# Attention and a gated feed-forward layer on one core: downward products three units behind instead of two, and the 64-key tile multiplied on 128 rows

## The chip, the cores and the metric

The kernel runs on one core of one Trainium2 chip. The metric is the device time of one execution in microseconds (us). The core has a matrix engine (PE, whose weight loads the profile lists apart as PEld), a vector engine (DVE), a scalar engine (ACT), a third elementwise engine (POOL) and a queue for transfers (SP). Each engine works through its own list of instructions in order; semaphores make one engine wait for another.

## What is computed

```python
# q, k, v: (8 batches, 8 heads, 576 positions, 64)
scores = q @ k.T / 8
mask = block_i >= block_j            # blocks of 64 positions, causal by block
attn = softmax(where(mask, scores, -1e9))
out = attn @ v                        # -> x: 4608 tokens x 512
h = x @ w_in                          # 512 -> 2048
g = h * erf(softplus(h))
result = g @ w_out                    # 2048 -> 512, float32
```

## The kernel before

**Attention** runs head by head (64 heads). For each head the scores are formed twice: once with queries on the rows, to find each row's maximum (`maxes`, L391 and L394), and once with keys on the rows (`probs`, L437 and L438), whose exponentials (L442) are the probabilities. The 576 keys make five tiles: four of 128 keys and one (`j` = 4) of 64. For two heads together `pv` multiplies the probabilities with the values (L486, output columns 64) and with a block of ones (L509, output columns 32), which gives the sums of the rows. The operand `V` holds one float32 array for the first three batches (`len(vv) == 1`), and from batch 3 on a high and a low float16 half (`len(vv) == 2`). There the lower 64 rows of the key tile of 64 are zero in the value array (padded on the host) and in the staged probabilities (a fill with zeros at L293). `min(P, S - j * P)` is the number of rows of the tile that the products of `pv` use: 128, and 64 for `j` = 4.

**The feed-forward layer** works on 18 tiles `t` of 256 tokens. The hidden 2048 are 16 slices of 128, two of which make a unit `u`; slices 0 to 7 are group 0 (units 0 to 3) and 8 to 15 group 1 (units 4 to 7). There are 144 units; `m16_4` in a name is tile 16, unit 4. A unit has three stages:

- up (L182): 24 products of 256 columns into one PSUM bank `h`;
- the gate (`gate`, L151 to L159): on ACT a tanh (L151) and two squares (L152, L153), on DVE four steps (L154 to L157, the last of which is the last reader of `h`), on ACT the rounding to float16 `gh` (L158), on POOL the rest `gl` (L159);
- down (L191): 12 products of 512 columns with `gh` and `gl` as the stationary operand, into the two output banks `o` of the tile.

`moe1` hands out these steps a few at a time between the steps of attention. It puts the up products of a unit together with the downward products of a unit that is `LAG` units older, in one merged list:

```python
downs.append(d)
lists.append((up, 0, 1))
if len(downs) > LAG or not jobs and downs:
    lists.append((downs.pop(0), 0, 1))
todo.extend(merged(*lists))
```

A scheduler then sets the order of each engine's list when the program is built, from the order of writing, priorities and times of its own; at run time each engine keeps to its list. While attention lasts, `h` has two banks (`ps_h`); once it is done, four (`ps_h2` is added), and only units of the feed-forward layer are left. Weights arrive as float64 and are converted in the first 20 heads or so (`to_f32`, `split_w`); the scale of each weight group comes from a small product `wt` (L125), which waits for a sum over all converted slices of the group (`wrs`, L123).

The lines on buffers: `mpool` has three buffers for each tag, so `gh`, `gl`, `r0` and `r1` have three each. `r0` and `r1` are the two float32 intermediates of the gate.

Of the kernel before, what the change touches and what calls it, by code (L numbers as in the profile page):

```python
# [8 lines left out]
F16 = mybir.dt.float16  # L9
F32 = mybir.dt.float32  # L10
# [22 lines left out]
def tile_attention_moe(ctx: ExitStack, tc: tile.TileContext, qk, v, w, maskrows, sels, out):  # L33
    nc = tc.nc
    B, H, D4, S = qk.shape
# [3 lines left out]
    P = 128  # L39
# [15 lines left out]
    cpool = ctx.enter_context(tc.tile_pool(name="cpool", bufs=1))  # L55
    wpool = ctx.enter_context(tc.tile_pool(name="wpool", bufs=1))
    xpool = ctx.enter_context(tc.tile_pool(name="xpool", bufs=2))
    mpool = ctx.enter_context(tc.tile_pool(name="mpool", bufs=3))
# [4 lines left out]
    make_identity(nc, ident)  # L63
    ones32 = cpool.tile([P, 32], F16, name="ones32")
    nc.gpsimd.memset(ones32, 1.0)
    ones = cpool.tile([P, P], F32, name="ones")
    nc.gpsimd.memset(ones, 1.0)
    bias = {}

    def const(val):  # L70
        if val not in bias:
            t = cpool.tile([P, 1], F32, name=f"c{len(bias)}")
            nc.gpsimd.memset(t, val)
            bias[val] = t
        return bias[val]
# [66 lines left out]
    def gate(h, name, t, g):  # L142

        nu = h.shape[1]
        n = nu * T
        flat = h.rearrange("p a b -> p (a b)")
        gh, gl = (mpool.tile([P, n], F16, tag=t_, name=f"{name}_{t_}") for t_ in ("gh", "gl"))
        r0, r1 = (mpool.tile([P, n], F32, tag=t_, name=f"{name}_{t_}") for t_ in ("r0", "r1"))
        r0s = r0.rearrange("p (a b) -> p a b", b=T)
        for b, lo, hi in spans(t * T, T):  # L150
            nc.scalar.activation(r0s[:, :, lo:hi], h[:, :, lo:hi], AF.Tanh, bias=const(p1), scale=bss[b][g][:, 0:1])  # L151
        nc.scalar.activation(r1, r0, AF.Square, bias=const(b1), scale=a1)  # L152
        nc.scalar.activation(r0, r1, AF.Square, bias=const(b2), scale=a2)  # L153
        nc.vector.scalar_tensor_tensor(out=r0, in0=r0, scalar=c3, in1=r0, op0=ALU.add, op1=ALU.mult)  # L154
        nc.vector.scalar_tensor_tensor(out=r0, in0=r1, scalar=c4, in1=r0, op0=ALU.add, op1=ALU.mult)  # L155
        nc.vector.scalar_tensor_tensor(out=r0, in0=r0, scalar=c5, in1=r0, op0=ALU.add, op1=ALU.mult)  # L156
        nc.vector.scalar_tensor_tensor(out=r0, in0=r0, scalar=fin, in1=flat, op0=ALU.add, op1=ALU.mult)  # L157
        nc.scalar.copy(gh, r0)  # L158
        nc.gpsimd.tensor_tensor(out=gl, in0=r0, in1=gh, op=ALU.subtract)  # L159
        return gh, gl  # L160

    def spans(t0, n):

        for b in range(t0 // S, (t0 + n - 1) // S + 1):
            yield b, max(0, b * S - t0), min(n, (b + 1) * S - t0)
# [49 lines left out]
            parts.append(x)  # L215
        return parts

    LAG = 2
    RATE = [12, 12, 28]
    done = []  # L220
    jobs = []
# [37 lines left out]
    def moe1(ready):  # L259
# [5 lines left out]
        if not todo:  # L265
            lists = []
            if jobs and len(done) >= 2 * jobs[0][2] + 2:
# [11 lines left out]
# [3 lines that stand above are left out]
# [4 lines left out]
    with tc.tile_pool(name="apool", bufs=2) as apool, tc.tile_pool(name="spool", bufs=1) as spool, \  # L286
# [14 lines left out]
        def bank(name):  # L301

            turn.append(0)
            k = len(turn) % 8 if not loaded else 0
            if k in (2, 5):
                return ps_h.tile([P, 512], F32, tag="h", name=name)
            if k in (3,):
                return ps_o.tile([P, 512], F32, tag="o", name=name)
            return ps_a.tile([P, 512], F32, tag="a", name=name)
# [151 lines left out]
        def pv(qd, pp, prs, V, usb, rs):  # L461

            vv = V[1:]
            terms = ((0, 0), (1, 0), (0, 1)) if len(vv) > 1 else ((0, 0),)
            one = ones32 if len(vv) > 1 else ones[:, :32]
            st = {}

            def ranges(q0, q1):

                for j in range(5):  # L470
                    if starts[j] < q1:
                        a = max(q0, starts[j])
                        pt, c = offs[j]
                        c += a - starts[j]
                        yield j, min(P, S - j * P), a - q0, pt, slice(c, c + q1 - a)

            def go(hf, j0, j1):
                q0, q1 = halves[hf]
                todo = list(ranges(q0, q1))
                if j0 == 0:  # L480
                    st[hf] = bank(f"u{qd}_{pp}_{hf}")
                u = st[hf]
                for j, kk, a, pt, cs in todo[j0:j1]:
                    for iv, ip in terms:
                        for hd in range(2):
                            nc.tensor.matmul(u[64 * hd : 64 * hd + 64, a : q1 - q0], lhsT=vv[iv][:kk, 2 * pp + hd, j, :], rhs=prs[hd][pt][ip][:kk, cs],  # L486
                                             start=j == 0 and (iv, ip) == terms[0], stop=j == todo[-1][0] and (iv, ip) == terms[-1])
                if j1 >= len(todo):
                    nc.scalar.copy(usb[:, q0:q1], u[:, : q1 - q0])


            order = []
            for hf, (q0, q1) in enumerate(((0, SH), (SH, S))):
                at, todo = 0, list(ranges(q0, q1))
                for n_, (j, kk, a, pt, cs) in enumerate(todo):
                    for k in range(len(vv)):
                        first, last = n_ == 0 and k == 0, n_ == len(todo) - 1 and k == len(vv) - 1
                        for hd in range(2):
                            order.append((at, hf, hd, k, kk, a, q1 - q0, pt, cs, first, last))
                        at += q1 - q0 - a  # L500
            order.sort(key=lambda o: o[0])

            def sums(n0, n1):
                if n0 == 0:
                    st["us"] = bank(f"us{qd}_{pp}")
                u = st["us"]
                for _, hf, hd, k, kk, a, w_, pt, cs, first, last in order[n0:n1]:
                    g = 2 * hf + hd
                    nc.tensor.matmul(u[32 * g : 32 * g + 32, a:w_], lhsT=one[:kk, :], rhs=prs[hd][pt][k][:kk, cs], start=first, stop=last)  # L509
                if n1 >= len(order):  # L510
                    nc.scalar.activation(rs[:, : S - SH], u[:, : S - SH], AF.Identity, bias=eps)
                    nc.scalar.activation(rs[:64, S - SH :], u[:64, S - SH : SH], AF.Identity, bias=eps[:64])

            return [lambda: go(0, 0, 2), lambda: sums(0, len(order)), lambda: go(1, 0, 5)]

        known = []
# [58 lines left out]
        vs, prs, usbs = {}, {}, {}  # L575
# [69 lines left out]
        for n in range(N + 3):  # L645
# [19 lines left out]
            if n % 2 == 0 and 2 <= n <= N:  # L665
                j = n // 2 - 1
                qd, pp = divmod(j, 2)
                usbs[j] = apool.tile([P, S], F32, tag="usb", name=f"usb{j}", bufs=2)
                steps = pv(qd, pp, [prs.pop(2 * j), prs.pop(2 * j + 1)], vs[qd], usbs[j], rss[j % 3])
                lists.append((late("pv", steps), 0, 1))  # L670
                if pp == 1:
                    normals[n + 1] = qd
# [60 lines left out]
```

## Time and profile before

| | |
|---|---|
| median of 3 runs | 1327.11 us (1323.97 to 1327.33) |
| profiled execution | 1333.15 us, of which the span of the core's instructions is 1331.3 us |
| mean granted PE clock | 0.973 of full speed |
| busy: PE, PEld, DVE, ACT, POOL | 1221.1, 804.8, 892.5, 784.6, 520.5 us |
| start of the first and last downward product | 164.6 and 1327.0 us |
| last product of attention (L566) | 1128.7 us |

The prediction quotes the rows themselves. In a row of a group, the columns are line, engine, operation, names and shapes, count, then busy time and mean duration of one in ns, then the engine's idle time just before such instructions and who ended it. In a row of waits they are who waited for whom, the time in total, the number of times and the longest. In a row of the timeline they are the start, the duration (over the whole of a merged run of instructions), engine, line, operation, count, and in brackets the idle time before it and who ended it. Ends of matrix products are modelled: a downward product shows some 0.38 us even where the next starts 0.22 us after it.

### The profile page before, as it was taken

What the parts mean: (1) busy time and instruction counts of PE and PEld (TensorE: products, weight loads), DVE (VectorE), ACT (ScalarE), POOL (GpSimd) and SP (SyncE); (2) the same over time, 40 slices, a digit from 0 to 9 for tenths busy, and PEclk for the clock granted to TensorE, in tenths of its full rate; (3) what the DMA queues carried; (4) which work ended last, traced back from release to release, by engine and by line L of the source; (5) the groups of instructions that cost most, each with busy time, mean ns of one, the idle gap of its engine ahead of it and who ended that gap; (6) DMA issues with size and microseconds to landing.
All of it is one profiled execution on the core that took longest, in us unless ns stands there. A gap on an engine that the chain in (4) does not pass through costs nothing. (4 is left out here: it accounts for less than half of the span.)

```text
span 1331.3 us, 23618 instructions
## 1 busy us (share of the span) xinstructions
PE 1221.1 (92%) x9108; PEld 804.8 (60%) x9108; DVE 892.5 (67%) x1583; ACT 784.6 (59%) x1555; POOL 520.5 (39%) x486
## 2 busy tenths in 40 slices
PE   1899898979999999999999999999999999999997
PEld 0455565556666676666666666667676666555553
DVE  4773887758567777686667766776778755554544
ACT  2453666557556676666666666666666675555553
POOL 4445445424434353534435343534343232222121
PEclk9899899779999999999999999999999999999999
DMA  9786568533444445454444544444434121211111
GB/s 264 190 215 149 128 180 198 146 94 91 119 114 108 121 121 123 112 114 110 101 129 104 123 113 108 117 125 107 120 97 111 55 66 37 86 56 48 64 48 48
DMA packets 95808, 151.74 MB, mean 114 GB/s; under 512 B 7804, under 2 KB 44988, under 8 KB 95696
## 3 DMA queue, kind: packets, MB, share of 16 engines
q1 hardware_dynamic: 69840, 93.34, 24.1%
q0 software_dynamic: 25216, 56.73, 20.0%
q8 instruction: 72, 1.18, 0.4%
q14 instruction: 40, 0.33, 0.1%
q10 hardware_dynamic: 640, 0.17, 0.1%
HBM read 121.73 MB, written 28.31 MB: 113 GB/s over the span
## 5 line engine op out<-in xcount | busy, mean ns | idle before, releaser
L182 PE MATMUL m_h<-xh,w 128*128 128x256 f16 x2304 | 474.2, 275 | 6.4 <-DVE m_r L157 5.2
L182 PEld LDWEIGHTS <-w 128*128 128x128 f16 x3456 | 326.7, 99 | 137.6 <-issue 17.6
L191 PE MATMUL o<-w,m_gh 128*128 128x512 f16 x1152 | 334.0, 387 | 27.4 <-ACT m_gh L158 25.2
L159 POOL TENSOR_TENSOR m_gl<-m_r,m_gh 128x512 f16<-128x512 f32 x144 | 174.7, 1213 | 424.1 <-ACT m_gh L158 382.5
L182 PE MATMUL m_h<-xl,w 128*128 128x256 f16 x1152 | 316.4, 275 | 0.9 <-DMA xl<-x_d 0.9
L394 DVE TENSOR_REDUCE mx<-s 64x1 f32<-64x288 f32 (+4 forms) x384 | 173.9, 470 | 122.6 <-PE s L391 121.6
L154 DVE SCALAR_TENSOR_TENSOR m_r<-m_r 128x512 f32<-128x512 f32 x144 | 113.4, 787 | 174.1 <-ACT m_r L153 171.7
L191 PE MATMUL o<-w,m_gl 128*128 128x512 f16 x576 | 205.1, 385 | 12.5 <-POOL m_gl L159 12.1
L442 ACT ACTIVATE p<-t 128x288 f32<-128x288 f32 (+4 forms) x384 | 145.9, 386 | 116.8 <-PE t L438 112.3
L437 PE MATMUL t<-qk 69*128 69x288 f32 (+4 forms) x384 | 165.9, 433 | 9.8 <-DMA qk<-mt 4.2
L151 ACT ACTIVATE m_r<-m_h,c,bs 128x512 f32<-128x512 f32 (+3 forms) x192 | 124.4, 667 | 83.8 <-PE m_h L182 81.4
L158 ACT CAST m_gh<-m_r 128x512 f16<-128x512 f32 x144 | 88.6, 615 | 144.0 <-DVE m_r L157 141.7
L391 PE MATMUL s<-qk 68*128 68x256 f32 (+3 forms) x384 | 147.6, 418 | 27.5 <-DVE mx L394 14.2
L379 POOL TENSOR_TENSOR qk<-st,qk 64x576 fp32r<-64x576 f32 x64 | 95.3, 1489 | 164.2 <-DMA qk<-qk 147.2
L191 PEld LDWEIGHTS <-m_gh 128*128 128x128 f16 x1152 | 95.8, 99 | 102.7 <-ACT m_gh L158 45.3
L155 DVE SCALAR_TENSOR_TENSOR m_r<-m_r,m_r 128x512 f32<-128x512 f32 x144 | 122.3, 849 | 3.3
L438 PE MATMUL t<-qk 128*128 128x288 f32 (+4 forms) x384 | 120.7, 315 | 0.0
L156 DVE SCALAR_TENSOR_TENSOR m_r<-m_r 128x512 f32<-128x512 f32 x144 | 115.5, 802 | 2.7
L454 DVE TENSOR_TENSOR p<-p,p 128x832 f16<-128x832 f32 x80 | 81.8, 1022 | 50.0 <-ACT p L453 49.7
L380 POOL TENSOR_TENSOR qk<-st,qk 64x576 fp32r<-64x576 f32 x64 | 98.7, 1542 | 26.9 <-DMA qk<-qk 22.9
L153 ACT ACTIVATE m_r<-m_r,c 128x512 f32<-128x512 f32 x144 | 103.7, 720 | 3.3 <-ACT m_r L152 1.2
L152 ACT ACTIVATE m_r<-m_r,c 128x512 f32<-128x512 f32 x144 | 103.7, 720 | 2.2 <-ACT p L442 0.6
(94 smaller groups left out, 1478.2 us busy)
## 6 DMA issues: line engine op xcount, KB each, us to landing
qk<-qk POOLq DMA_DIRECT2D x64, 432.0 KB, 4.9
st<-qk SPq DMA_DIRECT2D x64, 288.0 KB
qk<-qk POOLq DMA_DIRECT2D x64, 288.0 KB, 5.4
raw<-w SPq DMA_DIRECT2D x32, 512.0 KB
v<-v SPq DMA_DIRECT2D x16, 640.0 KB
x_d<-xs POOLq DMA_DIRECT2D x32, 288.0 KB, 2.7
xh<-x_d SPq DMA_DIRECT2D x36, 256.0 KB
xl<-x_d SPq DMA_DIRECT2D x36, 256.0 KB
```

What stands on the lines that cost most here:

```text
L151: nc.scalar.activation(r0s[:, :, lo:hi], h[:, :, lo:hi], AF.Tanh, bias=const(p1), scale=bss[b][g][:, 0:1])
L154: nc.vector.scalar_tensor_tensor(out=r0, in0=r0, scalar=c3, in1=r0, op0=ALU.add, op1=ALU.mult)
L155: nc.vector.scalar_tensor_tensor(out=r0, in0=r1, scalar=c4, in1=r0, op0=ALU.add, op1=ALU.mult)
L156: nc.vector.scalar_tensor_tensor(out=r0, in0=r0, scalar=c5, in1=r0, op0=ALU.add, op1=ALU.mult)
L159: nc.gpsimd.tensor_tensor(out=gl, in0=r0, in1=gh, op=ALU.subtract)
L182: nc.tensor.matmul(h[:, k, :], lhsT=wf[:, a, sl], rhs=x[:, cc, :], start=cc == 0 and i == 0, stop=cc == NCC - 1 and i == 2)
L191: nc.tensor.matmul(o[c], lhsT=a[:, sl], rhs=wf[:, b_, :], start=u == u0 and k == 0 and not lo and b_ == 2, stop=u == u1 - 1 and k == nu - ...
L391: nc.tensor.matmul(dst[:r, :w_], lhsT=qh[:K, i * P : i * P + r], rhs=kh[:K, k0 : k0 + w_], start=True, stop=True)
L394: nc.vector.tensor_reduce(out=mx[:r, col : col + 1], in_=src, axis=AX.X, op=ALU.max, negate=True)
L437: nc.tensor.matmul(s[:kk, :w_], lhsT=kh[:K, ks], rhs=qh[:K, q0 : q0 + w_], start=True, stop=False)
L438: nc.tensor.matmul(s[:kk, :w_], lhsT=klh[:, ks], rhs=qhl[:, q0 : q0 + w_], start=False, stop=True)
L442: nc.scalar.activation(p32s[part][:kk, c : c + w_ - skip], s[:kk, skip:w_], AF.Exp, scale=SCALE)
```

## The change

`LAG` goes from 2 to 3: the downward products of a unit are merged with the up products of the third unit after it. `gh` and `gl` get `LAG + 1` = 4 buffers, `r0` keeps 3, `r1` goes from 3 to 2. In `pv`, for batches 3 to 7, the key tile of 64 keys is multiplied on all 128 rows; its sums use a new block `ones32t` whose lower 64 rows are zero, set up by two fills on POOL at the start.

```diff
+    ones32t = cpool.tile([P, 32], F16, name="ones32t")
+    nc.gpsimd.memset(ones32t, 0.0)
+    nc.gpsimd.memset(ones32t[: S % P], 1.0)
...
-        gh, gl = (mpool.tile([P, n], F16, tag=t_, name=f"{name}_{t_}") for t_ in ("gh", "gl"))
-        r0, r1 = (mpool.tile([P, n], F32, tag=t_, name=f"{name}_{t_}") for t_ in ("r0", "r1"))
+        gh, gl = (mpool.tile([P, n], F16, tag=t_, name=f"{name}_{t_}", bufs=LAG + 1) for t_ in ("gh", "gl"))
+        r0, r1 = (mpool.tile([P, n], F32, tag=t_, name=f"{name}_{t_}", bufs=k) for t_, k in (("r0", 3), ("r1", 2)))
...
-    LAG = 2
+    LAG = 3
...
-            one = ones32 if len(vv) > 1 else ones[:, :32]
+            one, tail = (ones32, ones32t) if len(vv) > 1 else (ones[:, :32],) * 2
...
-                        yield j, min(P, S - j * P), a - q0, pt, slice(c, c + q1 - a)
+                        yield j, min(P, S - j * P) if len(vv) == 1 else P, a - q0, pt, slice(c, c + q1 - a)
...
-                            order.append((at, hf, hd, k, kk, a, q1 - q0, pt, cs, first, last))
+                            order.append((at, hf, hd, k, j, kk, a, q1 - q0, pt, cs, first, last))
...
-                for _, hf, hd, k, kk, a, w_, pt, cs, first, last in order[n0:n1]:
+                for _, hf, hd, k, j, kk, a, w_, pt, cs, first, last in order[n0:n1]:
...
-                    nc.tensor.matmul(u[32 * g : 32 * g + 32, a:w_], lhsT=one[:kk, :], rhs=prs[hd][pt][k][:kk, cs], start=first, stop=last)
+                    nc.tensor.matmul(u[32 * g : 32 * g + 32, a:w_], lhsT=(one if j < 4 else tail)[:kk, :], rhs=prs[hd][pt][k][:kk, cs], start=first, stop=last)
```

The counts of instructions stay what they were on every engine, but for the two fills on POOL. Nearly every list is reordered, and lines behind the new three are numbered 3 higher (L191 is L194). Three places matter below.

On PE, after attention, the first downward product of unit `m16_4` (its operand is `gh`) stands behind these rows before (`h` is the output of up products):

```order
L182 MATMUL m16_6_h_14850<-xh1_16_14528,w12_106 128x256
L182 LDWEIGHTS w12_106
L182 MATMUL m16_6_h_14850<-xl1_16_14530,w12_106 128x256
L191 LDWEIGHTS m16_4_gh_14780
L191 MATMUL o1_16_0_14738<-w8_102,m16_4_gh_14780 128x512
```

After the change it stands here:

```order
L185 MATMUL m16_6_h_14835<-xl1_16_14521,w13_110 128x256
L185 LDWEIGHTS w13_110
L185 MATMUL m16_6_h_14835<-xh1_16_14519,w13_110 128x256
L194 LDWEIGHTS m16_4_gh_14771
L194 MATMUL o1_16_0_14729<-w8_105,m16_4_gh_14771 128x512
```

Both stand among products of `m16_6`, but before it is near the start of that unit's up products, and after at their end: between the last up product of `m16_4` and this row lie 29 up and 13 downward products before, and 48 and 25 after.

On ACT, in the same stretch, the gates before (L158 is the rounding, which waits for DVE; L151, L152 and L153 open the next gate; L234 reads the output banks of a finished tile):

```order
L234 ACTIVATE ob0_17_1_14847<-o0_17_1_14524,bs7_0_129 128x512
L158 CAST m16_4_gh_14780<-m16_4_r0_14782 128x512
L151 ACTIVATE m16_5_r0_14836<-m16_5_h_14794,c1_88,bs7_1_130 128x512
L152 ACTIVATE m16_5_r1_14837<-m16_5_r0_14836,c2_90 128x512
L153 ACTIVATE m16_5_r0_14836<-m16_5_r1_14837,c3_92 128x512
L151 ACTIVATE m16_6_r0_14888<-m16_6_h_14850,c1_88,bs7_1_130 128x512
L158 CAST m16_5_gh_14834<-m16_5_r0_14836 128x512
L152 ACTIVATE m16_6_r1_14889<-m16_6_r0_14888,c2_90 128x512
```

and after:

```order
L161 CAST m16_4_gh_14771<-m16_4_r0_14773 128x512
L154 ACTIVATE m16_5_r0_14823<-m16_5_h_14785,c1_91,bs7_1_133 128x512
L155 ACTIVATE m16_5_r1_14824<-m16_5_r0_14823,c2_93 128x512
L156 ACTIVATE m16_5_r0_14823<-m16_5_r1_14824,c3_95 128x512
L237 ACTIVATE ob0_17_0_14854<-o0_17_0_14514,bs7_0_132 128x512
L237 ACTIVATE ob0_17_1_14888<-o0_17_1_14515,bs7_0_132 128x512
L161 CAST m16_5_gh_14821<-m16_5_r0_14823 128x512
L154 ACTIVATE m16_6_r0_14877<-m16_6_h_14835,c1_91,bs7_1_133 128x512
```

The rounding stands in one of four places: ahead of the next gate's tanh, inside it (where the tanh is cut in two at a batch's edge), behind it, or behind the first square. Over the last 32 steps from one unit to the next (of 144 units), the list after the change has 12, 7, 9 and 4 of these. The reading of the output banks moved one unit later.

On PE near the end of the weight conversion, the product `wt1` stood behind the up products of `m2_0` and `m2_1` and ahead of the scores of head 19:

```order
L182 MATMUL m2_1_h_2666<-xl0_2_2583,w3_97 128x256
L182 LDWEIGHTS w3_97
L182 MATMUL m2_1_h_2666<-xh0_2_2581,w3_97 128x256
L125 MATMUL wt1_2780<-wrs1_2778,ones_84 128x2
L437 MATMUL t0_19_0_2797<-qk3_134 128x288
L438 MATMUL t0_19_0_2797<-qk3_134 128x288
```

Now it stands ahead of both, behind the scores of head 18:

```order
L440 MATMUL t2_18_256_2766<-qk2_136 128x320
L441 MATMUL t2_18_256_2766<-qk2_136 128x320
L128 MATMUL wt1_2801<-wrs1_2799,ones_87 128x2
L440 MATMUL t0_19_0_2818<-qk3_137 128x288
L441 MATMUL t0_19_0_2818<-qk3_137 128x288
L394 MATMUL s01_21_2822<-qk1_135 128x256
L185 LDWEIGHTS w0_97
L185 MATMUL m2_0_h_2622<-xh0_2_2581,w0_97 128x256
```

The last two conversions that `wt1` waits for moved as well: on ACT they stood behind the tanh of `m2_0`, and now stand ahead of the exponentials of head 18.

## The prediction

> **What bounds the kernel now.** I read the first part of the page, then the waits by stretch of time, then the timeline of PE and ACT in the part after attention.
>
> ```profile
> PE 1221.1 (92%) x9108; PEld 804.8 (60%) x9108; DVE 892.5 (67%) x1583; ACT 784.6 (59%) x1555; POOL 520.5 (39%) x486
> ```
>
> PE is the fullest engine, so what it waits for is what can be won. Its waits from 300 to 1106 us, where attention and feed-forward run mixed, are led by these:
>
> ```profile
> PE o L191 <- ACT m_gh L158: 14.5, 23, 1.9
> PE o L191 <- POOL m_gl L159: 8.9, 11, 1.5
> PE m_h L182 <- DVE m_r L157: 4.4, 6, 2.7
> PE rb L566 <- ACT rw L561: 2.0, 2, 1.3
> ```
>
> So 23.4 us in 34 stalls are downward products that wait for their gate; everything from attention is small. A stall costs more than its idle time, because the modelled ends hide part of it. The timeline of PE after attention shows the price of one product and of a stall:
>
> ```profile
> 1182.50 0.27 PE L182 MATMUL m_h<-xh,w 128*128 128x256 f16 x1
> 1183.05 1.04 PE L191 MATMUL o<-w,m_gh 128*128 128x512 f16 x4 [0.27 <-ACT m_gh L158]
> 1184.34 0.39 PE L191 MATMUL o<-w,m_gl 128*128 128x512 f16 x1 [0.26 <-POOL m_gl L159]
> ...
> 1187.39 0.27 PE L182 MATMUL m_h<-xh,w 128*128 128x256 f16 x1
> 1189.90 0.27 PE L182 MATMUL m_h<-xh,w 128*128 128x256 f16 x1
> ...
> 1316.95 1.90 PE L191 MATMUL o<-w,m_gh 128*128 128x512 f16 x8 [0.77 <-ACT m_gh L158]
> ```
>
> Between 1187.39 and 1189.90 lie 23 steps of up products: 2.51/23 = 0.109 us each. Eight downward products take 1.90, of which the last shows 0.38: (1.90 - 0.38)/7 = 0.217 each. A unit is then 24 x 0.109 + 12 x 0.217 = 5.22 us of PE. At 1182.50 the next product could start at 1182.61 and starts at 1183.05: 0.44 us lost where 0.27 shows idle. I add 0.38 - 0.217 = 0.163 us to each stall of a downward product.
>
> After attention the units take longer than 5.22 us. The roundings of the gate (L158), one for each unit, from 1135 us to the end:
>
> ```profile
> L158 ACT CAST m_gh<-m_r x33: 600/617/618, 1135.9 to 1322.2; 128x512 f16<-128x512 f32 x33
> ```
>
> That is (1322.2 - 1135.9)/32 = 5.82 us for a unit. Two things could set it, and the timeline of ACT shows the second:
>
> ```profile
> 1166.38 0.60 ACT L158 CAST m_gh<-m_r 128x512 f16<-128x512 f32 x1
> 1166.89 0.72 ACT L153 ACTIVATE m_r<-m_r,c 128x512 f32<-128x512 f32 x1
> ...
> 1171.44 0.61 ACT L158 CAST m_gh<-m_r 128x512 f16<-128x512 f32 x1
> ...
> 1176.50 0.62 ACT L158 CAST m_gh<-m_r 128x512 f16<-128x512 f32 x1 [3.07 <-DVE m_r L157]
> 1177.02 0.77 ACT L151 ACTIVATE m_r<-m_h,c,bs 128x512 f32<-128x512 f32 x1
> ...
> 1182.37 0.62 ACT L158 CAST m_gh<-m_r 128x512 f16<-128x512 f32 x1 [3.07 <-DVE m_r L157]
> ...
> 1194.72 0.61 ACT L158 CAST m_gh<-m_r 128x512 f16<-128x512 f32 x1
> ...
> 1200.27 0.62 ACT L158 CAST m_gh<-m_r 128x512 f16<-128x512 f32 x1
> ```
>
> ACT stands idle for 3.07 us until DVE is through, and does not begin the next gate, which stands behind L158 in its list. So the gates themselves form a loop, whose length hangs on where L158 stands: ahead of the next tanh 1182.37 - 1176.50 = 5.87 us; inside a tanh cut in two 1200.27 - 1194.72 = 5.55; behind the tanh 1176.50 - 1171.44 = 5.06; behind the first square, from the parts, 0.51 (to the start of L153) + 0.72 + 3.07 = 4.30.
>
> **The change, part by part.**
>
> *Downs three units behind, after attention.* From the last up product of a unit to its first downward one, PE had 29 up and 13 downward products to do (the first pair of lists above): 29 x 0.109 + 13 x 0.217 = 5.98 us. The gate needs from the start of its tanh (1177.02) to the end of rounding (1182.37 + 0.62) 5.97 us, so any delay stalls PE, and a stalled PE makes the next up products late, which makes ACT wait for them. With 48 and 25 products the distance is 10.66 us, 4.7 more than the gate needs: these stalls go. What is late next is the gate loop. In the list after the change the last 32 steps are 12, 7, 9 and 4 of the four kinds: 12 x 5.87 + 7 x 5.55 + 9 x 5.06 + 4 x 4.30 = 172.0 us, against 186.3 measured. This loop cannot be hidden at the end, because the last gate precedes the last product. I add 2 us, for three finished tiles whose outputs ACT reads (L234) between L153 and L158, at the 0.68 us of the first of these groups each:
>
> ```profile
> L234 ACT ACTIVATE ob<-o,bs 128x512 f32<-128x512 f32 x32 | 21.8, 682 | 13.5 <-PE o L191 10.7 <-DMA qk<-mt 1.8 <-PE t L438 0.8
> L159 POOL TENSOR_TENSOR m_gl<-m_r,m_gh 128x512 f16<-128x512 f32 x144 | 174.7, 1213 | 424.1 <-ACT m_gh L158 382.5 <-issue 29.3 <-ACT p L442 10.5
> L182 PEld LDWEIGHTS <-w 128*128 128x128 f16 x3456 | 326.7, 99 | 137.6 <-issue 17.6 <-DVE m_r L157 5.5
> ```
>
> Gain 186.3 - 174 = 12 us. If PE alone were the bound: 186.3 - 32 x 5.22 = 19 us. I take 12, since the loop is read from rows.
>
> *The same during attention.* The stalls on `gl` are worth 8.9 + 11 x 0.163 = 10.7 us, those on `gh` 14.5 + 23 x 0.163 = 18.2, together 29. Here the bank `h` has two buffers, and the up products of the second unit after it stand in PE's list 24 up and 14 downward products behind (in the median), about where the downward ones stood before (24 and 13). So a late gate now stops PE at `h`, released by L157, instead of at `gh`, released by L158. L157 is earlier by the 0.62 us of L158, and earlier than `gl` by that and by POOL's 1.21 us (L159) more. The mean `gl` stall (8.9/11 = 0.81) is shorter than 1.83, so those 10.7 us go. The mean `gh` stall is 14.5/23 = 0.63 idle, just what goes; they are uneven (up to 1.9), so I take two thirds, 12. Then attention has less slack behind PE: I give back 5 us, as much again as its small waits make now. Gain 18, between 0 (everything comes back at `h`) and 29 + 4.4 = 33.
>
> *The weight conversion.* PE had this stall and a slow clock around it (the row of the 50 us has the granted clock as 0.76):
>
> ```profile
> 283.66 0.59 PE L125 MATMUL wt<-wrs,ones 128*128 128x2 f32 x2 [5.43 <-DVE wrs L123]
> 250.00:300.00 50.00, 40.53 (x232) 25.70 (x232) 31.23 (x74) 25.77 (x57) 17.67 (x17) 0.76 0.47 123
> ACT a L112 <- DMA raw<-w: 29.5, 12, 13.3
> ```
>
> `wt1` and the conversions ahead of it now stand before the up products of `m2_0`, which had to wait for their input; the stall of 5.43 us should shrink to below 1. But now ACT can be stopped at L112 by a weight still on its way, with exponentials behind it, and such a wait was up to 13.3 us. I take a gain of 4, between a loss of 13 and a gain of 10 (the stall, and half of the 12 us that 24% of 50 us lost to the clock).
>
> *128 rows for the 64-key tile.* Rows of PE and PEld at the two places where 64-row products follow 128-row ones:
>
> ```profile
> 831.13 0.46 PE L486 MATMUL u<-p,v 128*64 128x192 f16 x8
> 831.30 0.17 PEld L486 LDWEIGHTS <-v 64*64 64x64 f16 x6
> 825.17 0.41 PE L509 MATMUL us<-p,ones 128*32 128x192 f16 x8
> 825.35 0.11 PEld L509 LDWEIGHTS <-ones 64*32 64x32 f16 x4
> L486 PEld LDWEIGHTS <-v 128*64 128x64 f16 x720 | 36.4, 110 | 18.7 <-issue 12.8 <-PE t L438 1.1
> L486 PEld LDWEIGHTS <-v 64*64 64x64 f16 x120 | 3.4, 106 | 2.9
> ```
>
> The last pair of 128 rows starts at 831.13 and needs 192/512 x 0.217 = 0.08 us, but the first load for 64 rows comes at 831.30: 0.09 us lost; at 825.17 the last pair needs 0.05 (128 columns) and the load comes 0.18 later: 0.13. Loads within a shape run ahead of the products; these wait. The 20 pairs of heads in float16 have two such places each: 40 x 0.11 = 4 us. The products keep their columns, so they cost the same; a load of 128 rows takes 4 ns more, 200 x 4 ns = 1 us at most if none is hidden. Gain 4, between -1 and 40 x 0.18 = 7.
>
> [...]
>
> *Buffers and fills.* `r1` with two buffers: L152 of unit u+2 needs L155 of u done; L158 of u, which follows L155, stands ahead of it in every case of ACT's list, so nothing. `gh` and `gl` with four keep the margin that three had. The two fills stand on POOL ahead of the first loads of scores, which PE waits for; the like fill takes 0.12 us:
>
> ```profile
> 0.88 0.12 POOL L65 MEMSET ones<- 128x32 f16 x1
> ```
>
> Loss 0.2.
>
> *Sum.* 12 + 18 + 4 + 4 - 0.2 = 38 us off the profiled 1333.15 us (span 1331.3): 1295. The median of the runs is 0.45% below that execution, so 1289.
>
> **Rivals.**
>
> *PE alone is the bound.* If ACT falls behind without harm, the part after attention gains 19, the mixed part 29: 19 + 29 + 4 + 4 = 56, 1277, scaled 1271. For it: the distance of 10.66 us leaves 4.7 us in which the loop may lag. Against: the loop's 172 us must end before the last product.
>
> [...]
>
> ```profile
> 1150.00:1200.00 50.00, 46.73 (x312) 29.26 (x310) 27.83 (x40) 23.14 (x38) 9.25 (x8) 1.00 0.17 53
> ```
>
> Loads are busy for 29.26/50 = 59%, while a unit at 5.22 us has 36 loads of 99 ns (L182), 68%: room for 14%, where the products' 93% would leave 7%.
>
> *The waits come back at `h` and in attention.* All `gh` stalls of the mixed part turn into waits for `h`, and attention's own waits grow: mixed part 5, after attention 10, conversion 0, rows 2: 17, 1316, scaled 1310. For it: the places in PE's list are equal, as counted. Against: L157 is 0.62 us ahead of L158.
>
> *Slower: `h` with two banks holds everything.* Where no attention stands between, 24 up and 14 downward products are 24 x 0.109 + 14 x 0.217 = 5.65 us, and a gate up to L157 takes 5.97 - 0.62 = 5.35. If the gates of the mixed part, queued among exponentials on ACT and maxima on DVE, slip because PE no longer pauses for them, every up product waits, with all of attention's products behind it on PE. The 38 us are undone at 38/102 = 0.37 us for each of the 102 units from the tenth to the end of attention; at 0.5 us it is 13 us slower, 1340. Against: this wait now is 4.4 us in 6 places, and the median has 25 products of attention between.
>
> *Nothing happens* (within 0.3%, about 4 us, which a measurement of this kernel can't tell from no change): the gate stalls move and the conversion loses its 13 us.
>
> **Chances.** Forecast (1275 to 1305) 0.55; PE alone (below 1275) 0.13; waits come back (1305 to 1322) 0.17; nothing 0.05; slower 0.10. Below 1264 all stalls and the clock's share would have to be won, above 1320 only the last two lie: the range is 1264 to 1320. Faster 0.55 + 0.13 + 0.17 = 0.85, same 0.05, slower 0.10.
>
> **What the profile after would show.** Waits of L194 for L161 and L162 near zero; L161 after attention at 172 to 176 us for 32 steps, and ACT idle behind DVE, not behind PE's up products; PE's wait of L185 for L160 grown from 5 to about 10 us; no stall over 2 us at L128; no rows of 64*64 and 64*32 in float16. I am wrong if L185 waits for L160 beyond 25 us, if the steps of L161 stay at 5.8 us, or if a new long wait stands before 300 us.

## The result and the profile after

The changed kernel takes 1287.99 us (median of 4 runs, 1282.45 to 1288.71), the kernel before 1327.22 in the same comparison (4 runs, 1323.97 to 1329.58): ratio 0.9692, 95% interval 0.9659 to 0.9726. The prediction was 1289.0 us. The profiled execution took 1288.4 us, its span is 1286.6. The kernel of before was profiled in a run 6 us above its median, so the spans differ by 44.7 us, the medians by 39.2. In the experiments, two runs that lie more than 1.5% above the fastest of their kernel (1340.89 us and 1816.39 us) are left out of the medians and ratios.

The busy time of the page after, beside the row of before in the prediction:

```profile
PE 1200.5 (93%) x9108; PEld 810.2 (63%) x9108; DVE 895.8 (70%) x1583; ACT 780.5 (61%) x1555; POOL 523.6 (41%) x488
```

PE's busy time fell by 20.6 us with the same number of products: part of a wait counts as busy (the prediction has 0.44 us lost where 0.27 shows idle), and a product at a low clock counts for longer (0.213 us at a granted clock of 0.50 instead of 0.109, in the last section).

To see where the time went, both spans are cut at the same work. Attention normalises its sums 16 times (a reciprocal on DVE); the cuts are the 4th, the 5th and the 16th of these. The columns are the stretch, its length, the busy times of PE, PEld, DVE, ACT and POOL with their counts, the granted PE clock, the DMA share and GB/s. Before:

```profile
0.00:245.41 245.41, 200.06 (x1293) 120.88 (x1294) 164.91 (x329) 127.93 (x308) 114.57 (x123) 0.92 0.76 187
245.41:322.38 76.97, 65.80 (x420) 41.73 (x420) 56.53 (x116) 46.02 (x98) 29.80 (x26) 0.84 0.41 104
322.38:1122.42 800.04, 765.56 (x6172) 525.99 (x6171) 566.30 (x989) 506.62 (x987) 331.27 (x298) 1.00 0.43 107
1122.42:1331.30 208.88, 189.72 (x1229) 116.21 (x1227) 104.73 (x152) 104.01 (x164) 44.81 (x39) 0.99 0.18 57
```

After:

```profile
0.00:250.61 250.61, 204.87 (x1289) 122.68 (x1290) 168.31 (x333) 128.30 (x310) 114.18 (x125) 0.90 0.74 183
250.61:315.78 65.17, 59.11 (x421) 39.41 (x420) 54.61 (x115) 43.32 (x94) 30.72 (x27) 0.92 0.51 124
315.78:1087.99 772.21, 753.48 (x6178) 528.50 (x6177) 567.49 (x985) 506.62 (x991) 334.85 (x299) 1.00 0.44 111
1087.99:1286.60 198.61, 183.10 (x1224) 119.65 (x1222) 105.35 (x152) 102.29 (x160) 43.86 (x38) 0.99 0.18 59
```

The start lost 5.2 us, the stretch with the end of the weight conversion won 11.8, the mixed part 27.8, the end 10.3: 44.7 in all. The waits of PE in the mixed part, the longest first:

```profile
PE m_h L185 <- DVE m_r L160: 11.2, 16, 1.6
PE u L489 <- DVE p L457: 4.3, 7, 0.9
```

The downward products (L194) no longer wait there for their gate, and what is late next is the bank `h`, as forecast: 11.2 us where the kernel before had 4.4. After attention, first the kernel before (from 1106 us), then the changed one:

```profile
PE o L191 <- ACT m_gh L158: 10.1, 21, 3.1
PE o L191 <- POOL m_gl L159: 2.9, 12, 0.3
```

```profile
PE o L194 <- DVE pt L235: 6.4, 4, 2.6
PE o L194 <- ACT ob L237: 2.5, 3, 1.7
PE o L194 <- ACT m_gh L161: 1.1, 1, 1.1
```

The gate waits are nearly gone here too, but downward products now wait for the output banks of the tile before, until DVE (L235) or ACT (L237) has read them. That wait was not in the prediction. And the roundings, from 1095 us to the end, with ACT's waits beside them:

```profile
L161 ACT CAST m_gh<-m_r x33: 607/618/620, 1099.1 to 1278.8; 128x512 f16<-128x512 f32 x33
```
```profile
ACT m_gh L161 <- DVE m_r L160: 63.4, 29, 3.2
ACT m_r L154 <- PE m_h L185: 20.4, 14, 2.8
```

32 steps take 179.7 us, 5.62 each: below the 186.3 of before, above the 172 to 176 of the forecast. ACT waits mostly for DVE, as forecast, and for 20.4 us for PE's up products, where it waited 47.8 us for them in the kernel before (17 times, from 1136 us).

### The profile page after: what moved, and what is told of

It reads as the page before. It is cut to its first block, busy times and chain, and to the rows that moved or that the text cites. A ratio compares the mean times of both kernels' runs of the same rounds, so it can differ in the third digit from the quotient of the medians.

```text
span 1286.6 us, 23640 instructions
## 1 busy us (share of the span) xinstructions
PE 1200.5 (93%) x9108; PEld 810.2 (63%) x9108; DVE 895.8 (70%) x1583; ACT 780.5 (61%) x1555; POOL 523.6 (41%) x488
## 4 chain that ended last, share of the span: by engine, by line
PE 49%; DVE 26%; ACT 14%; DMA 5%; issue 4%; POOL 1%; SPq 0%; DVEq 0%; POOLq 0%; ACTq 0%
PE m_h L185 14%; PE o L194 14%; DVE m_r L158 5%; DVE m_r L157 5%; PE u L489 4%; DVE m_r L159 4%; DVE m_r L160 3%; PE t L440 3%; ACT m_r L155 3%; ACT m_r L154 3%; PE s L394 3%; ACT m_r L156 3%; PE t L441 3%; DVE mx L397 2%; PE us L512 2%
## 5 line engine op out<-in xcount | busy, mean ns | idle before, releaser
L194 PE MATMUL o<-w,m_gh 128*128 128x512 f16 x1152 | 337.0, 382 | 10.5 <-DVE pt L235 6.4
L194 PE MATMUL o<-w,m_gl 128*128 128x512 f16 x576 | 206.0, 384 | 0.3 <-POOL m_gl L162 0.3
L161 ACT CAST m_gh<-m_r 128x512 f16<-128x512 f32 x144 | 88.8, 617 | 192.0 <-DVE m_r L160 187.9
L394 PE MATMUL s<-qk 68*64 68x288 f32 (+3 forms) x384 | 150.9, 424 | 27.4 <-DVE mx L397 14.9
L382 POOL TENSOR_TENSOR qk<-st,qk 64x576 fp32r<-64x576 f32 x64 | 95.9, 1498 | 149.4 <-DMA qk<-qk 136.2
L194 PEld LDWEIGHTS <-m_gh 128*128 128x128 f16 x1152 | 98.5, 98 | 67.2 <-issue 19.7
L158 DVE SCALAR_TENSOR_TENSOR m_r<-m_r,m_r 128x512 f32<-128x512 f32 x144 | 120.6, 837 | 2.8
L383 POOL TENSOR_TENSOR qk<-st,qk 64x576 fp32r<-64x576 f32 x64 | 103.1, 1611 | 30.0 <-DMA qk<-qk 27.1
L457 DVE TENSOR_TENSOR p<-p,p 128x832 f16<-128x832 f32 x80 | 82.6, 1033 | 36.3 <-ACT p L456 36.2
```

The costliest lines, as they stand in the source:

```text
L194: nc.tensor.matmul(o[c], lhsT=a[:, sl], rhs=wf[:, b_, :], start=u == u0 and k == 0 and not lo and b_ == 2, stop=u == u1 - 1 and k == nu - ...
L394: nc.tensor.matmul(dst[:r, :w_], lhsT=qh[:K, i * P : i * P + r], rhs=kh[:K, k0 : k0 + w_], start=True, stop=True)
```

## The experiments

The kernels that ran together share the runs of the kernel before: the first four a median of 1330.89 us (20 runs), the next four 1326.24 (7), the last three 1330.48 (7). Each edit is against the changed kernel. Where an expectation counts the normalisations from zero, its "3rd to 4th" and "4th to 16th" are the two middle rows above.

**The new distance alone.**

```diff
-                        yield j, min(P, S - j * P) if len(vv) == 1 else P, a - q0, pt, slice(c, c + q1 - a)
+                        yield j, min(P, S - j * P), a - q0, pt, slice(c, c + q1 - a)
...
-                    nc.tensor.matmul(..., lhsT=(one if j < 4 else tail)[:kk, :], ...)
+                    nc.tensor.matmul(..., lhsT=one[:kk, :], ...)
```

> Downs three behind with its buffers, but the 64-key tile on 64 rows as before. If the 0.11 us at each of 40 places counts on the path, this is about 4 us slower than the changed kernel: 1292. If PE has slack at those places, or the rows only reorder the lists: 1288, the same as the changed kernel. Either way the rows of 64*64 and 64*32 in float16 are back.

Measured: 1288.19 us (4 runs), ratio 0.9681 (0.965 to 0.9713). The total cannot be told from the changed kernel's. The mixed part of the profile:

```profile
309.85:1090.73 780.88, 757.94 (x6178) 527.69 (x6177) 568.81 (x986) 506.46 (x991) 334.36 (x299) 1.00 0.45 110
```

800.04 - 780.88 = 19.2 us belong to the distance; the 128 rows would be the remaining 8.7 (780.88 - 772.21).

**The 128 rows alone.** `LAG` 2 and three buffers for `r1`.

> The 64-key tile on 128 rows alone, downs two behind with three buffers of everything. If the drain between shapes is on the path: 4 us faster than before, 1323. If PE, which waits for gates behind those places, only waits longer there: 1327, the same as before.

Measured: 1332.24 us (11 runs), ratio 1.0006 (0.9975 to 1.0038): no gain that can be told. Its mixed part is 794.63 us, 5.4 shorter than before, and its granted clock 0.971 on average of its runs, against 0.975 in the 34 runs of the kernel before that were taken with the experiments. Among those 34, a clock higher by 0.01 goes with a time shorter by 10.4 us (a straight line through them), so the difference would be worth some 4 us, about what the rows won, if the clock is the cause there. Whether the edit itself lowers the clock, or the reordered lists of the first 250 us, was not tested; the total shows no gain from the rows.

Where the rows change something directly, the timeline of PE shows it (start, duration, line). A pair of heads with 30 products and its successor, before and after:

```profile
829.72 1.87 PE L486 MATMUL u<-p,v 128*64 128x320 f16 x30
831.52 0.28 PE L182 MATMUL m_h<-xh,w 128*128 128x256 f16 x1
```
```profile
802.23 1.75 PE L489 MATMUL u<-p,v 128*64 128x320 f16 x30
803.91 0.39 PE L194 MATMUL o<-w,m_gl 128*128 128x512 f16 x1
```

From start to successor 1.80 us became 1.68. For the 32 products that make the sums, 0.94 us (824.58 to 825.52) became 0.83 (797.21 to 798.04): together 0.23 for a pair of heads, 20 x 0.23 = 4.6 us, where the prediction had 4. So what the expectation calls the drain between shapes was worth 0.12 and 0.11 us at the two places.

**The distance of three after attention alone, two before.**

```diff
-            if len(downs) > LAG or not jobs and downs:
+            if len(downs) > (LAG if len(hpools) > 1 else LAG - 1) or not jobs and downs:
```

> The changed kernel with downs two behind as long as attention lasts and three behind after it. By the split between the two profiles (34 us up to the last normalisation, 10 us after it) this gives back the stalls of the mixed part: 4 for the rows and 10 for the end are left of the gain, about 1313. If the end's gain came only because the mixed part handed over in better order, it is nearer to 1323.

Measured: 1323.32 us (9 runs), ratio 0.9944 (0.9908 to 0.998). In the profile the end takes 1318.6 - 1117.99 = 200.6 us, 8.3 less than before, and the mixed part 795.79, where the rows alone had 794.63. The total fell by only 7.6 us against the kernel before, not by the 14 of the expectation's first case, and its number is that of the second. The stretches decide between the two: the end's gain is there without the mixed part's. The two halves of the distance are separate gains.

**The reverse, first attempt.** The same line, with `LAG if len(hpools) == 1 else LAG - 1`.

> The reverse: three behind while attention lasts, two behind after it. Theory: only the end's gain of 10 us is lost, 1298. If the end's loop of gates is set by ACT's list alone, so that the distance on PE does not matter there, it stays at 1288 to 1290.

Measured: 1290.99 us (4 runs), ratio 0.9706 (0.9671 to 0.974), end 199.7 us. The edit did not do what it was meant to: for each unit put into `downs` one is taken out, so a smaller bound reached with the queue already full leaves the distance at three. It stands as a repeat of the changed kernel: its mixed part of 772.53 us is the changed kernel's 772.21, and its stretch from the 4th to the 5th normalisation takes 70.38 us where that had 65.17.

**The reverse, mended.** The first unit after attention takes two downs together.

```diff
-            if len(downs) > LAG or not jobs and downs:
-                lists.append((downs.pop(0), 0, 1))
+            lag = LAG if len(hpools) == 1 else LAG - 1
+            if len(downs) > lag or not jobs and downs:
+                both = downs.pop(0)
+                if jobs and len(downs) > lag:
+                    both = both + downs.pop(0)
+                lists.append((both, 0, 1))
```

> Three behind while attention lasts, and two behind after it: at the first unit after attention two units' downward products are put beside one unit's up products, so that the distance does shrink (in the earlier try one was taken for each unit put in, and the distance stayed three). If the distance matters after attention: the gate stalls are back there and the end takes 8 to 10 us longer, 1296 to 1298. If the loop of gates sets the end's time whatever the distance: 1288 to 1291.

Measured: 1296.37 us (3 runs, 1287.16 to 1298.44), ratio 0.9747 (0.9699 to 0.9794). The end is 1294.6 - 1085.8 = 208.8 us, that of before, and the gate waits are back:

```profile
PE o L194 <- ACT m_gh L161: 9.8, 20, 3.1
PE o L194 <- POOL m_gl L162: 2.4, 10, 0.3
```

So the distance after attention is worth 8 to 10 us, shown from both sides (8.3 where it is added alone, 10.2 where it is taken away).

**Four output banks after attention.** Are the new waits for L235 and L237 the bound of the end?

```diff
+    opools = [ps_o]
-                    os[g, t] = [ps_o.tile(...)]
+                    os[g, t] = [opools[len(os) % len(opools)].tile(...)]
...
+            tc.tile_pool(name="ps_o2", bufs=2, space=PSUM) as ps_o2:
+        opools.append(ps_o2)
```

> The changed kernel with four output banks instead of two for tiles that begin after attention, in banks that attention has left. In the changed kernel PE waits after attention for the readers of those banks (L235 on DVE 6.4 us in 4 waits, L237 on ACT 2.5 in 3), since the gates lag and the readers stand behind them in their lists. If these waits set the end's time: some 9 us faster, 1279. If the loop of gates sets it, PE only runs ahead and waits for gates instead: 1286 to 1288.

Measured: 1290.13 us (4 runs), ratio 0.9727 (0.9698 to 0.9756); the end is 198.6 us, as without it. The waits for the banks are gone and PE waits for the rounding in their place (the line numbers are 1 higher):

```profile
PE o L195 <- ACT m_gh L161: 9.2, 11, 2.0
```

The 32 steps of L161 take 179.7 us here too. The bank waits were a sign of the late gates, not a bound.

**The rounding on DVE after attention.** It takes the wait for DVE out of ACT's list, and with it the loop.

```diff
-        nc.scalar.copy(gh, r0)
+        (nc.vector.tensor_copy if len(hpools) > 1 else nc.scalar.copy)(gh, r0)
```

> The changed kernel with the rounding of the gate (L161) on DVE instead of ACT for units that begin after attention, so ACT no longer stands waiting for DVE with the next gate behind it. If the loop through ACT and DVE sets the end's time (5.62 us a unit measured, 5.38 from the list): the steps fall towards PE's 5.22, 32 x 0.4 = up to 13 us faster, 1275 to 1282. If the output banks set it: 1288, with the waits for L235 as they are.

Measured: 1281.54 us (4 runs), ratio 0.9652 (0.9609 to 0.9694). The end is 186.6 us, 12.0 less, with next to no waits of PE (the largest is in the second fence):

```profile
L161 DVE CAST m_gh<-m_r x29: 408/427/429, 1132.2 to 1277.5; 128x512 f16<-128x512 f32 x29
```
```profile
PE m_h L185 <- DVE m_r L160: 1.4, 3, 0.7
```

(1277.5 - 1132.2)/28 = 5.19 us for a unit: the 5.22 that the prediction worked out for PE alone. So the loop of gates bound the end of the changed kernel.

**Both.**

> Both edits. If PE alone is left as the bound after attention: 32 x 5.22 = 167 us for the steps that take 180 in the changed kernel, 1275. If either edit alone gives that, this gives no more than the better of the two.

Measured: 1277.09 us (4 runs, 1276.22 to 1278.49), ratio 0.962 (0.9599 to 0.9642): the best of all, with the same end of 186.6 us (1274.4 - 1087.83). The extra banks add nothing at the end; that its median is 4.5 us below the kernel with the rounding alone comes from elsewhere. The first 4 normalisations took 254.9 us in that kernel's profile and 242.8 in this one, and its 4 runs spread from 1275.69 to 1286.87.

**A third bank for `h` during attention**, taken from attention's four (`ps_h` 3, `ps_a` 3). Are the 11.2 us of waits for `h` to be had?

> The changed kernel with a third bank for h while attention lasts, taken from attention's own four banks (ps_a three instead of four). In the changed kernel PE waits 11.2 us in 16 stalls for L160 to free h. If that wait is what is left to win in the mixed part: the stretch from the 4th to the 16th normalisation falls from 772 to about 760, the whole to 1276. If attention lives on its fourth bank: its waits grow instead (L394 and L440 for L397 and L445), and the time is 1288 or more.

Measured: 1301.47 us (4 runs, 1290.69 to 1302.32), ratio 0.9759 (0.9697 to 0.9821). From 330 to 1090 us PE's waits for L160 are gone from the head of its list, and attention's stand there (the next is L489 for L457, 6.9 us):

```profile
PE t L440 <- DVE mx L397: 7.9, 7, 2.0
```

The mixed part is 786.95 us, 14.7 longer than in the changed kernel, and above all five other profiles with two banks and edits that act only after attention (769.7 to 775.6). The bank costs more there than the waits it removes.

**The distance of three only after the second weight group is scaled.** It leaves `wt1` behind the up products of `m2_1`, where it stood before.

```diff
-            if len(downs) > LAG or not jobs and downs:
+            if len(downs) > (LAG if scaled[1] else LAG - 1) or not jobs and downs:
```

> Downs two behind until the weights of the second group are scaled, then three. The list of PE has the product wt1 behind the up products of m2_0 and m2_1 again, as before the change. If that place makes PE's wait for the sum (5.4 us before, 1.0 after): the wait of some 6 us is back, the stretch from the 3rd to the 4th normalisation takes 76 to 77 us instead of 65 to 72, and the whole is 5 to 10 us slower than the changed kernel, 1293 to 1298. If the stretch was faster for another reason: 1288. In either case the mixed part after it stays at 772.

Measured: 1299.08 us (4 runs, 1294.74 to 1305.07), ratio 0.9771 (0.9723 to 0.9819). Its wait at `wt1` and its stretch from the 4th to the 5th normalisation, with the granted clock ahead of the last two columns:

```profile
PE wt L128 <- DVE wrs L126: 6.3, 1, 6.3
```
```profile
249.92:326.08 76.16, 66.33 (x428) 42.69 (x427) 56.39 (x118) 47.13 (x101) 30.28 (x27) 0.82 0.43 106
```

The stall is back, the clock as low as before (0.82, and 0.84 there), and the stretch as long as before (76.97), while the mixed part keeps its gain (776.53 us); the total is somewhat above the expected 1293 to 1298. The two other kernels with a distance of two at that point, the rows alone and the distance after attention alone, have the stall too (6.2 and 6.3 us) and stretches of 76.77 and 76.28 us. So the order of the early lists is what shortened that stretch.

**Three buffers for `gh` and `gl`, and for `r1`**, with the distance of three.

> Downs three behind, but gh and gl with three buffers and r1 with three. The rounding of unit u then needs the downward products of unit u-3 done, which stand beside the up products of u. If they end before the rounding is due (the gate reaches it 5.35 us after the last up product): nothing lost, 1288. If not, ACT and POOL wait for PE, and the gates come later: a few us slower, 1292 or more, most of it after attention.

Measured: 1286.79 us (4 runs, 1283.75 to 1292.63), ratio 0.9681 (0.9635 to 0.9726). The fourth buffer does nothing here. In the stretch of the conversion (70.75 us) its profile shows what stands in place of the stall at `wt1`:

```profile
PE m_h L185 <- DMA xl<-x_d: 5.0, 1, 5.0
```

The profiles of the other seven kernels that keep the distance there have a wait for this input too (4.1 to 5.7 us in six of them, in one 2.6 and 3.7 for the two halves of the input), and stretches of 69.1 to 71.6 us; the profile of the changed kernel has no such wait, and 65.17 us. So 65.17 is the favourable end, and 5 to 8 us is the usual gain.

## Why the prediction was right

**The end: 12 forecast, 10.3 measured.** The mechanism is shown: with the distance back the end is back to 208.8 us, and without the loop it falls to 186.6. The term that was mis-sized is the loop: 172.0 + 2 us were forecast for 32 steps, 179.7 measured. The timeline of ACT after the change shows the kind of step that was wrong:

```profile
1126.77 0.62 ACT L161 CAST m_gh<-m_r 128x512 f16<-128x512 f32 x1 [3.07 <-DVE m_r L160]
...
1133.65 0.62 ACT L161 CAST m_gh<-m_r 128x512 f16<-128x512 f32 x1 [0.54 <-DVE m_r L160]
1134.17 0.72 ACT L156 ACTIVATE m_r<-m_r,c 128x512 f32<-128x512 f32 x1
...
1138.38 0.62 ACT L161 CAST m_gh<-m_r 128x512 f16<-128x512 f32 x1 [1.03 <-DVE m_r L160]
```

and that of DVE why:

```profile
1130.29 0.74 DVE L235 SCALAR_TENSOR_TENSOR pt<-o,bs,pt 128x512 f32<-128x512 f32 x1
...
1132.28 0.74 DVE L235 SCALAR_TENSOR_TENSOR pt<-o,bs,pt 128x512 f32<-128x512 f32 x1
1132.94 0.68 DVE L160 SCALAR_TENSOR_TENSOR m_r<-m_r,m_h 128x512 f32<-128x512 f32 x1
1134.99 1.11 DVE L157 SCALAR_TENSOR_TENSOR m_r<-m_r 128x512 f32<-128x512 f32 x1 [1.38 <-ACT m_r L156]
```

A rounding behind the first square (four of 32) makes the step after it short, 1138.38 - 1133.65 = 4.73, which I had put at 4.30 from the parts. But it stands there where DVE reads two output banks of a finished tile (L235) between the four steps of the gate, and the step before it takes 6.88 us instead of 5.87. The four steps before are 6.88, 6.55, 6.87 and 6.88, each 1.0 us above the price of its kind (5.87, 5.55, 5.87 and 5.87), together 4.0; the four after are 4.73 to 4.76, together 1.8 us above 4.30. That is 5.8 of the 7.7 us by which 179.7 exceeds 172.0. Most of the other 1.9, about what the 2 us had been added for, lies in one step with an output read on ACT (6.58 instead of 5.87) and in three where a tanh cut in two stands behind the rounding as a whole (6.11 or 6.12). I had added the tile's outputs as ACT reads them (L234) and left out DVE's. This is read from the trace; no run took these reads away alone.

**PE alone as the bound (0.13)** was the wrong case for this kernel, and right about what lies behind it: once the loop is gone, a unit takes 5.19 us. In the profile of both edits, PEld is busy for 33.91 of the 50 us from 1150, 68% as worked out, where the kernel before had 59%:

```profile
1150.00:1200.00 50.00, 50.00 (x349) 33.91 (x348) 32.92 (x52) 25.45 (x40) 10.44 (x9) 1.00 0.19 64
```

The prediction's two estimates of the room were 7% from the products' 93% and 14% from the loads' 59%; 5.82 us for a unit became 5.19, 11% less, which lies between the two. Which of the two shares tells the room better isn't shown.

**The mixed part: 18 for the distance and 4 for the rows forecast, 27.8 measured.** The distance alone gave 19.2. The waits for `gl` and `gh` are gone, and the wait for `h` grew from 4.4 to 11.2 us, as the forecast's "about 10" said. The 5 us given back for attention were not needed in full: attention's own waits are 6.7 us in this profile, and were 5.3. The rows gave 5.4 at a distance of two and 8.7 at three, where the bursts account for 4.6 in the whole kernel. In the profile of the distance alone attention's own waits are 10.4 us, 3.7 more than in that of the changed kernel, which with the 4.6 makes most of the 8.7; whether the rows caused that difference isn't shown. The mixed part takes 769.7 to 775.6 us in the profiles of the five kernels whose edits act only after attention, so single profiles don't settle what lies between 4.6, 5.4 and 8.7.

**The conversion: 4 forecast, 11.8 in this profile, 5 to 8 in most.** The stall at `wt1` fell from 5.43 to 1.0 us, and the kernel that leaves the distance at two until then has it back, 6.3 us, and a stretch of 76.16. What the prediction did not see is which transfer comes late in its place: not a weight (L112) but the input of `m2_0` (`xl`), 4 to 6 us in most profiles. One of its signs of being wrong was a new long wait before 300 us: the profile of the changed kernel has none, but all eight others that keep the distance there have this one. By that sign the account of this part was incomplete, though the stretch was shorter in all of them. Of the 11.8 us, 6.7 are PE's shorter busy time (65.80 to 59.11) at a clock of 0.92 instead of 0.84, and 5.1 less idle time; the prediction had half of the clock's loss in its bound of 10 and little of it in its 4.

**The start: 0 forecast, -5.2 measured.** The changed kernel and those whose edits act only after attention reach the 4th normalisation after 238.9 to 254.9 us, the changed kernel after 250.6, the kernel before after 245.4. The 5.2 us lie within this spread. Most of the spread lies between the 1st and the 4th, 148.7 to 160.4 us, the shortest at a clock of 0.97, the longest at 0.89.

**The slower rival (0.10)** asked for `h` to hold everything at 0.37 us a unit. The wait is 11.2 us in 16 places, 0.11 a unit over its 102 units. **The waits that come back (0.17)** came back at two fifths of what they were: 11.2 against 23.4 + 4.4.

The sum was right partly because its errors cancel: 38 us off against 44.7 in the profiled pair, with the end 1.7 too high, the conversion 7.8 and the mixed part 5.8 too low, and the start 5.2 to the other side. A second stroke of luck lies in the scaling: the sum gave 1295 for a profiled execution, which took 1288.4, and the 0.45% to the median took off 6 us, while the changed kernel's profiled execution lies 0.4 us from its median.

## What to carry over

When an engine with a list in fixed order waits in mid-list for another, look past the waiting consumer at the loop of producers: moving the consumer back won what the loop left, 10 us at the end, and taking the wait out of the list (the rounding on the engine that it waits for) won 12 more. When the lengths of such steps are added up, look for what the other engine does among them, here two reads of output banks, which made each of four steps 1.0 us longer than their price from other rows. And a wait that appears after a change isn't yet a bound: two more output banks removed 8.9 us of waits and not one of time.

## What the runs showed of the hardware

In the profile of the distance alone the granted clock falls twice from 1.00 to 0.50 around PE's waits, which my 4 us for the conversion had hardly counted. PE waits 1.95 and 5.02 us for the two halves of the input of `m2_0`, and works at a clock of 0.50 behind the second wait (the first fence is PE's timeline, the second has the granted clock ahead of the last two columns):

```profile
259.82 0.38 PE L185 MATMUL m_h<-xh,w 128*128 128x256 f16 x2 [1.95 <-DMA xh<-x_d]
...
265.81 0.37 PE L185 MATMUL m_h<-xl,w 128*128 128x256 f16 x1 [5.02 <-DMA xl<-x_d]
...
268.32 0.42 PE L185 MATMUL m_h<-xl,w 128*128 128x256 f16 x1
268.53 0.64 PE L185 MATMUL m_h<-xh,w 128*128 128x256 f16 x2
268.96 0.42 PE L185 MATMUL m_h<-xl,w 128*128 128x256 f16 x1
...
278.17 0.64 PE L440 MATMUL t<-qk 69*128 69x320 f32 x1 [1.88 <-DVE mx L397]
```
```profile
258.00:260.00 2.00, 0.18 (x3) 0.17 (x2) 0.41 (x3) 0.20 (x1) 0.21 (x1) 1.00 0.84 252
260.00:262.00 2.00, 0.79 (x6) 0.62 (x5) 1.64 (x12) 1.36 (x3) 0.00 (x0) 0.66 1.11 250
266.00:268.00 2.00, 2.00 (x11) 1.45 (x10) 0.00 (x0) 0.00 (x0) 1.51 (x2) 0.50 0.16 41
276.00:278.00 2.00, 0.28 (x2) 0.06 (x1) 2.00 (x4) 1.50 (x5) 0.00 (x0) 0.92 0.01 1
280.00:282.00 2.00, 2.00 (x11) 1.45 (x10) 2.00 (x5) 1.28 (x3) 1.81 (x3) 0.50 0.62 149
```

Three up products take 268.96 - 268.32 = 0.64 us, 0.213 each instead of 0.109. The drop of the clock came before the long wait: a single fall from 1.00 to 0.50 that gives a mean of 0.66 between 260 and 262 us lies at 260.64, and the wait of 5.02 us begins at 265.81 - 5.02 = 260.79. So the clock fell behind the wait of 1.95 us, and was still low when the work went on at 265.81. By the same working the second drop lies at 277.7, inside a wait of 1.88 us. Both drops came with gaps of PE below 2 us (1.95 and 1.88). In the rows just before or at the drops PE is busy for 0.18 and 0.28 of 2 us; no run varied this, so what lowers the clock stays open. Kernels with the same early lists differ from run to run in the start, as shown above; why they do was not tested.

In the profile of the changed kernel the first of DVE's four steps takes 1.11 us instead of 0.69 in the four gates that follow a rounding behind the first square, and 0.69 in the other 28. It starts at 1134.99 in the rows above, while POOL takes the rest of the gate before:

```profile
1134.40 1.16 POOL L162 TENSOR_TENSOR m_gl<-m_r,m_gh 128x512 f16<-128x512 f32 x1 [5.71 <-issue]
```

POOL's instruction goes on for 1134.40 + 1.16 - 1134.99 = 0.57 us after DVE's begins. In all four of these gates the two overlap by 0.56 or 0.57 us, in none of the other 28 at all. DVE's 0.42 us more are what a step behind such a rounding has above the forecast's 4.30. That the overlap causes them isn't shown: no run took it away.
